# A gated linear attention and two MLPs on one core: halves of 64 tokens, another order of the first transfers, measured durations in the planner

## The chip, the core and the metric

The kernel runs on one core of a Trainium2 chip. The metric is device time in microseconds (us) from one launch. TensorE (PE) multiplies; VectorE (DVE) and ScalarE (ACT) do the elementwise work; SyncE (SP) issues every transfer, in program order. Each engine executes its own instructions in the order in which they were written down for it, and waits on semaphores for the others.

## What is computed

```python
def _attn_ref(q, k, v, f_logit) -> np.ndarray:
    B, H, S, D = q.shape
    f = 1.0 / (1.0 + np.exp(-f_logit))
    state = np.zeros((B, H, D, D), dtype=np.float32)
    y = np.zeros_like(q)
    for t in range(S):
        state = f[:, :, t, :, None] * state + np.einsum('bhd,bhe->bhde', k[:, :, t], v[:, :, t])
        y[:, :, t] = np.einsum('bhd,bhde->bhe', q[:, :, t], state)
    return y.astype(np.float32)
...
def _moe_ref(x, w_in, w_out) -> np.ndarray:
    h = x @ w_in
    relu6 = np.clip(h + 3.0, 0.0, 6.0)
    g = h * relu6 / 6.0
    return (g @ w_out).astype(np.float32)
...
    attn_out = _attn_ref(**attn_kwargs)
    B, H, S, D = attn_out.shape
    x = np.ascontiguousarray(attn_out.transpose(0, 2, 1, 3)).reshape(B * S, H * D)
    x = _moe_ref(x=x, **moe_kwargs)
    return _moe2_ref(x=x, **moe2_kwargs)
```

B, H, S, D are 4, 8, 768, 48. The second MLP has `h * tanh(softplus(h))` between its two products. Both have 3072 tokens, 384 features and 2048 hidden units. The data are float32; the weights arrive as float64.

## The kernel before

The attention runs in 24 units `u` of 128 tokens of one batch (six units to a batch, so units 0, 6, 12 and 18 start with an empty state and units 5, 11, 17 and 23 have no successor). The eight heads stand in four pairs `p`, one head of a pair in partitions 0 to 47 and the other in 64 to 111. `attention` (L232) makes of a unit: decay logs (`exp`, `ln` on ACT, L249, L251), their running sums (for units 0 to 7 by matmuls with the triangle `tri`, `sum_up`, L258; for the others by a scan on DVE, L266), the scaled `k` and `q` (L269, L271), `scores` (L277: 8 matmuls of 128 columns, 48 rows deep), the masked scores `A` (L286), the transposed `k` (`turn`, L296, copied to `kn`), `outer` (L303: 16 matmuls of 48 columns, the product of k and v that goes into the state), and `values` (L320): 12 matmuls of 128 columns that multiply `q` with the old state `sd`, and 16 that multiply the masked scores with `v`, on top of them in the same PSUM bank. In units from 4 on, `outer` stands inside `values`. `carry` (L338) brings the state `st` to the unit's end, two ACT copies (L348) put it into `sd`. The unit's output is split into a high and a low part, `xh` and `xl` (L352, L353).

The MLPs run on six blocks of 512 tokens (four units), first MLP over all blocks, then the second. For each of 16 hidden slices `f`, `hidden` (L363) does 9 large matmuls of 128x128 by 512 columns into `h` (three products of high and low parts for each of three feature tiles), an activation `g` split into `gh` and `gl`, and 9 more large matmuls into the three `o` banks. Each weight slice of the first MLP comes as 768 KB of float64 (`raw`), is turned into float32 by two ACT and two DVE operations (`stream`, L205) through a single buffer `we` (`WE = 1`), and split by ACT into `wh` and by DVE into `wl` (`weight`). This happens in the first block; the weights stay in memory. The second MLP's weights are converted later and written to DRAM.

The order of the work on every engine is made by a planner (`Plan.emit`, L111) when the program is built: it plays the operations through with an assumed cost for each and, on an engine that comes free, takes of the operations that are ready at that moment the one with the lowest rank. The costs are the numbers in `act`, `dve`, `dma` and `pe` (L181 to L192). Whatever it finds ready in an idle moment is written into the engine's order at that place, and has to be executed there. Where it sees PE idle before the first hidden slice, it puts in dummy matmuls on `cap` (`warm`).

## Time and profile before

| | us |
|---|---|
| median of 3 runs | 913.21 (912.27 to 915.97) |
| the profiled execution | 913.63 |
| its span, first to last instruction | 911.8 |
| PE busy | 894.3 |
| DVE busy | 645.2 |
| ACT busy | 554.7 |

The profiled execution is 1.8 us longer than its span. A busy PE is not PE at its peak: its rows overlap, so the text counts from the start of one matmul to the start of the next. The granted TensorE clock is 0.999 of full speed (2.4 GHz) over the span. The stages: up to 36.7 us the first four units of attention without any hidden slice (the head), up to about 123 us the first block with the stream of weights, up to about 460 us the other blocks of the first MLP with units 8 to 23 between them, and from there the second MLP.

### The profile page before, as it was taken

Reading aid. Unit: us, or ns where it says so; the run is one execution under the profiler, and the core shown is the slowest. Engines: PE = TensorE matmul, PEld = TensorE weight load, DVE = VectorE, ACT = ScalarE, POOL = GpSimd, SP = SyncE. Lnnn points to the kernel's source line nnn. Section 1 sums busy time; section 2 is a strip of 40 time slices with the busy share of each in tenths; the row PEclk is TensorE's granted clock in tenths of the full one; section 3 lists DMA queues with packets and bytes.
Section 4 is the critical chain, followed back from the end, with each engine's and each line's share of the span. In section 5 each row is a group of like instructions: output and inputs, shape, how many; then the busy total and the mean of one; then the engine's idle time right before and its main releaser. Section 6 shows DMA issues by size and latency. Waiting matters only on the chain.

```text
span 911.8 us, 14717 instructions
## 1 busy us (share of the span) xinstructions
PE 894.3 (98%) x5945; PEld 732.8 (80%) x5945; DVE 645.2 (71%) x979; ACT 554.7 (61%) x943; POOL 0.2 (0%) x4
## 2 busy tenths in 40 slices
PE   9899899999999999999999999999999999999997
PEld 8777678888888878888888888888888888888785
DVE  3889977766655445543465878888888888876894
ACT  5888876757545444433454665766666666654673
POOL 0000000000000000000000000000000000000000
PEclk9999999999999999999999999999999999999999
DMA  9756656656412111200233300200100100000001
GB/s 267 221 183 207 199 176 230 202 194 230 135 55 77 52 44 42 79 13 1 72 103 93 116 1 1 70 1 6 65 1 12 58 1 13 35 1 0 36 1 38
DMA packets 30155, 75.86 MB, mean 83 GB/s; under 512 B 3456, under 2 KB 4736, under 8 KB 30080
## 3 DMA queue, kind: packets, MB, share of 16 engines
q1 hardware_dynamic: 30080, 74.86, 25.7%
q8 instruction: 48, 0.79, 0.4%
q14 instruction: 27, 0.22, 0.1%
HBM read 59.11 MB, written 15.73 MB: 82 GB/s over the span
## 4 chain that ended last, share of the span: by engine, by line
PE 89%; DVE 4%; ACT 3%; DMA 3%; issue 1%; SPq 0%; ACTq 0%
PE o L196 42%; PE h L196 28%; PE a L196 14%; PE m L196 5%; DMA raw<-w 1%; DMA f<-fn 1%; DVE we L216 1%; DMA o<-fn 1%; PE m L298 1%; DVE we L218 1%; ACT f L183 1%; ACT we L183 1%; DVE wl L199 1%; DVE gl L199 0%; ACT raw L183 0%
## 5 line engine op out<-in xcount | busy, mean ns | idle before, releaser
L196 PE MATMUL o<-gl,wh 128*128 128x512 f32 x570 | 223.0, 391 | 5.1 <-DVE gl L199 5.1
L196 PE MATMUL o<-gh,wh 128*128 128x512 f32 x570 | 226.3, 397 | 0.1
L196 PE MATMUL o<-gh,wl 128*128 128x512 f32 x570 | 222.3, 390 | 0.0
L196 PE MATMUL h<-xh,wh 128*128 128x512 f32 x402 | 158.3, 394 | 0.0
L196 PE MATMUL h<-xh,wl 128*128 128x512 f32 x402 | 156.7, 390 | 0.0
L196 PE MATMUL h<-xl,wh 128*128 128x512 f32 x402 | 156.5, 389 | 0.0
L391 DVE SCALAR_TENSOR_TENSOR g<-g,h 128x512 f32<-128x512 f32 x96 | 65.9, 686 | 117.6 <-ACT g L183 117.5
L196 PEld LDWEIGHTS o<-gl,wh 128*128 128x128 f32 x570 | 107.0, 188 | 28.8 <-DVE gl L199 7.8
L196 PEld LDWEIGHTS o<-gh,wh 128*128 128x128 f32 x570 | 107.0, 188 | 27.0 <-issue 3.0
L196 PEld LDWEIGHTS o<-gh,wl 128*128 128x128 f32 x570 | 107.0, 188 | 22.4
L183 ACT ACTIVATE g<-h,small 128x512 f32<-128x512 f32 x96 | 65.8, 686 | 96.8 <-PE h L196 91.9
L183 ACT ACTIVATE gh<-q 128x512 fp32r<-128x512 f32 x94 | 59.3, 631 | 75.1 <-DVE q L202 71.2
L183 ACT ACTIVATE gh<-g 128x512 fp32r<-128x512 f32 x96 | 60.5, 630 | 50.8 <-DVE g L391 50.8
L196 PEld LDWEIGHTS h<-xh,wl 128*128 128x128 f32 x402 | 75.5, 188 | 16.2 <-DVE wl L199 0.2
L196 PEld LDWEIGHTS h<-xh,wh 128*128 128x128 f32 x402 | 75.5, 188 | 15.9 <-issue 0.6
L199 DVE TENSOR_TENSOR gl<-g,gh 128x512 fp32r<-128x512 f32 x96 | 66.1, 689 | 30.6 <-ACT gh L183 30.1
L196 PEld LDWEIGHTS h<-xl,wh 128*128 128x128 f32 x402 | 75.5, 188 | 15.2
L183 ACT ACTIVATE q<-k,small 128x512 f32<-128x512 f32 x96 | 69.4, 723 | 19.5 <-DVE k L399 16.4
L183 ACT ACTIVATE k<-k 128x512 f32<-128x512 f32 x96 | 59.5, 625 | 32.4 <-DVE k L396 32.4
L202 DVE TENSOR_TENSOR q<-q,k 128x512 f32<-128x512 f32 x96 | 66.0, 688 | 15.3 <-ACT q L183 13.7
L199 DVE TENSOR_TENSOR gl<-q,gh 128x512 fp32r<-128x512 f32 x94 | 64.6, 688 | 7.7 <-ACT gh L183 6.8
L399 DVE SCALAR_TENSOR_TENSOR k<-k 128x512 f32<-128x512 f32 x96 | 65.3, 685 | 0.8 <-ACT k L183 0.7
(130 smaller groups left out, 1154.9 us busy)
## 6 DMA issues: line engine op xcount, KB each, us to landing
raw<-w SPq DMA_DIRECT2D x32, 768.0 KB, 4.6
v<-vn SPq DMA_DIRECT2D x24, 256.0 KB, 3.0
w<-we SPq DMA_DIRECT2D x16, 384.0 KB, 2.6
raw<-w SPq DMA_DIRECT2D x16, 384.0 KB, 3.0
k<-kt SPq DMA_DIRECT2D x23, 224.0 KB, 3.0
q<-qt SPq DMA_DIRECT2D x23, 224.0 KB, 3.6
x<-o SPq DMA_DIRECT2D x18, 256.0 KB, 2.3
f<-x SPq DMA_DIRECT2D x18, 256.0 KB, 2.7
```

The source lines that it names most:

```text
L183: lambda: nc.scalar.activation(out=out(), in_=in_(), func=func, **k), r, w)
L196: nc.tensor.matmul(**k)
L199: dve(n, rank, lambda: nc.vector.tensor_tensor(out=out(), in0=a(), in1=b().bitcast(F32), op=ALU.subtract), r, w)
L202: dve(n, rank, lambda: nc.vector.tensor_tensor(out=out(), in0=a(), in1=b(), op=ALU.mult), r, w)
L216: dve(768, rank, lambda: stt(out=eu(), in0=eu(), scalar=3, in1=v(0), op0=ALU.logical_shift_left, op1=ALU.bitwise_or), (e, raw, (raw, 0)), ...
L218: dve(768, rank, lambda: stt(out=eu(), in0=v(1), scalar=0x80000000, in1=eu(), op0=ALU.bitwise_and, op1=ALU.bitwise_or), (e, raw), (e,))
L298: nc.tensor.transpose(ztv()[:, p, :], k3()[:, p, :], ident[0:R, 0:R])
L391: dve(n, rank, lambda: nc.vector.scalar_tensor_tensor(out=gg(), in0=gg(), scalar=6.0, in1=zn(), op0=ALU.min, op1=ALU.mult), (g, z), (g,))
L399: dve(n, rank, lambda: nc.vector.scalar_tensor_tensor(out=ee(), in0=ee(), scalar=2.0, in1=ee(), op0=ALU.add, op1=ALU.mult), (e,), (e,))
```

## The change

Units from 8 on (`SPLIT`) are worked in two halves of 64 tokens. The scores are formed within each half only: 16 matmuls of 64 columns. The scaled `q` of one head and the masked scores of the same head stand above each other in the partitions of one tile `T` (`A`), and the state and `v` above each other in `v`, so that one matmul over up to 128 partitions gives both terms: `values` is 32 matmuls of 64 columns and the 12 of the state are gone. The second half needs the state in the middle of the unit: `outer` runs twice (32 matmuls; once in a last unit, which had none), with a copy of `v` whose second half is zero, and `middle` (two DVE operations) adds it to the state. The outer products now stand behind the scores in the same PE operation. The mask becomes four DVE operations of 64x256 in place of two of 128x512, the scaled `q` two in place of one. A last unit now also has a `turn`. New inputs are `vs` (512 KB a unit in place of 256 KB) and `vk` (384 KB a unit).

The first 21 transfers have an order written out by hand (`FIRST`). The planner's costs are other numbers. Some tiles share memory in another way (`kh`, `kl` are gone; two `A` are one).

```diff
+SPLIT = 8
+CC = C // 2
...
-CST_RANK = -12
+FIRST = "f0 tri k0 q0 f1 f2 ident v0 k1 q1 f3 v1 w0 k2 q2 v2 k3 q3 w1 v3 w2".split()
...
-    sd = const.tile([R, NP, PD], F32, name="sd")
...
+    sd = new("vk", [128, 2 * NP * PD], 2)
+    sdv = lambda: sd()[0:R, 0:NP * PD].rearrange("p (a b) -> p a b", a=NP)
...
-        P.op("act", 0.065 + n / 1200 + (0.09 if "accum_out" in k or "bias" in k and k["bias"] != 1.0 else 0), rank,
+        P.op("act", max(0.36, 0.03 + n / 1000) + (0.22 if "accum_out" in k else 0.04 if k.get("bias", 1.0) != 1.0 else 0), rank,
...
-        P.op("dve", 0.065 + n / (1920 if fast else 960), rank, fn, r, w)
+        P.op("dve", max(0.38 if n > 128 else 0.1, 0.065 + n / 960), rank, fn, r, w)
...
-        P.op("sp", max(0.65, size / 360e3), rank, lambda: nc.sync.dma_start(out=out(), in_=in_()), r, w,
+        P.op("sp", max(0.45, size / 280e3), FIRST.index(name) - 99 if name in FIRST else rank, lambda: nc.sync.dma_start(out=out(), in_=in_()), r, w,
...
+        if split:
+            w = new("vk", [128, 2 * NP * PD], 2)
+            wv = lambda i: w().rearrange("p (i a d) -> p i a d", i=2, a=2 * NP)[:, i]
+            dma(rk(1), w, lambda: vk[u - SPLIT], (), (w,), 128 * 3072)
+            dma(rk(3), v, lambda: vs[u - SPLIT], (), (v,), 128 * 4096)
+        else:
+            dma(rk(3), lambda: v()[:, 0:NP * 128], lambda: vn[u], (), (v,), 128 * 2048, f"v{u}")
...
-            dve(512, rk(1), lambda: nc.vector.tensor_tensor_scan(out=bf(), data0=cap, data1=fl(f)(), initial=0.0,
+            dve(1024, rk(1), lambda: nc.vector.tensor_tensor_scan(out=bf(), data0=cap, data1=fl(f)(), initial=0.0,
...
+        if split:
+            T = new("A", [128, 2 * 2 * NP * CC], 2)
+            Tv = lambda: T().rearrange("p (i c a t) -> p i c a t", i=2, c=2, a=NP)
+            chunks = lambda z, r0, r1: z()[r0:r1].rearrange("p (a c t) -> p c a t", a=NP, c=2)
+            own, other = ((0, HB), (HB, R)), ((HB, 128), (0, HB))
+            cols = ((0, D), (CC - D, CC))
+            for i, (r0, r1) in enumerate(own):
+                dve(512, rk(2), lambda i=i, r0=r0, r1=r1: nc.vector.tensor_tensor(
+                    out=Tv()[r0:r1, i], in0=chunks(q, r0, r1), in1=chunks(lambda: bf(), r0, r1), op=ALU.mult),
+                    (q, b), ((T, "q", i),))
...
+            pe(0.4, rk(3), turn, (k, "ident"), (zt,))
+            act(448, rk(3.5), lambda: flat(kn()), lambda: flat(ztv()), AF.Copy, (zt,), (kn,))
+            zs = [bank("a", [128, 512], 2) for i in range(2)]
+
+            def scores():
                 for p in range(NP):
+                    for c in range(2):
+                        t = slice(c * CC, c * CC + CC)
+                        for i, (r0, r1) in enumerate(SPANS):
+                            mm(out=zs[i]()[t, p * CC:(p + 1) * CC], lhsT=k3()[r0:r1, p, t], rhs=Tv()[r0:r1, i, c, p],
+                               start=True, stop=True)
+                for p in range(NP):
+                    for m in range(1 if last else 2):
+                        for g in range(0, R, 32):
+                            to = slice(g, min(g + 32, R))
+                            mm(out=zuv(m)[to, p, :], lhsT=kn()[:, p, to], rhs=wv(1 - m)[:, 2 * p + (g >= HB)],
...
+            pe(1.1, rk(4), scores, (k, kn, w, (T, "q", 0), (T, "q", 1)), (*zs, zu))
             if not first:
+                for i, (r0, r1) in enumerate(own):
+                    act(192, rk(3), lambda i=i, r0=r0, r1=r1: vv()[r0:r1, i, 0, :, cols[i][0]:cols[i][1]],
+                        lambda r0=r0, r1=r1: st[r0:r1], AF.Copy, ("st", v), ((v, 0, i),))
+            for i, (r0, r1) in enumerate(own):
+                def middle(i=i, r0=r0, r1=r1):
+                    to = vv()[r0:r1, i, 1, :, cols[i][0]:cols[i][1]]
+                    if first:
+                        nc.vector.tensor_copy(out=to, in_=zuv(0)[r0:r1])
+                    else:
+                        nc.vector.tensor_tensor(out=to, in0=st[r0:r1], in1=zuv(0)[r0:r1], op=ALU.add)
+
+                dve(192, rk(5), middle, (zu, v, *(() if first else ("st",))), ((v, 1, i),))
+            for c in range(2):
+                for i in range(2):
+                    def mask(i=i, c=c):
+                        t = slice(c * CC, c * CC + CC)
+                        nc.vector.tensor_tensor(
+                            out=Tv()[other[i][0]:other[i][1], i, c],
+                            in0=zs[i]()[t, 0:NP * CC].rearrange("p (a t) -> p a t", a=NP),
+                            in1=tri[t, t].unsqueeze(1).to_broadcast([CC, NP, CC]), op=ALU.mult)
+
+                    dve(256, rk(5.5 + c), mask, (zs[i], "tri"), ((T, i, c),))
...
+            zx = bank("a", [128, 512], 2)
...
+            def values():
+                for w in range(2):
+                    for c in range(2):
+                        for n in range(w, 3 * NP, 1 + 2 * w):
+                            p, j = divmod(n, 3)
+                            i, at = ((0, 0), (0, 32), (1, 32))[j] if not w else (1, 0)
+                            mm(out=zxv()[n % 4 * 32:n % 4 * 32 + 32, n // 4, c * CC:(c + 1) * CC],
+                               lhsT=vv()[0:(128, R)[i], i, c, p, at:at + 32], rhs=Tv()[0:(128, R)[i], i, c, p],
+                               start=(not w and not c and n < 4), stop=(j != 1 or w == 1), skip_group_check=True)
+
+            pe(1.0, rk(7), values, (v, *(((v, 0, i) for i in range(2)) if not first else ()), (v, 1, 0), (v, 1, 1),
+                                    (T, "q", 0), (T, "q", 1), *((T, i, c) for i in range(2) for c in range(2))), (zx,))
...
+        else:
+            mul(512, rk(2), fl(q), fl(q), bf, (q, b), (q,))
...
-        pe(9 * (0.003 + n / 2400), i - TAIL_LEAD * tail, run, [("w", f, 0), ("w", f, 1), *x_keys(ph, j, 0), *x_keys(ph, j, 1)], (z,))
+        pe(9 * (0.0135 + n / 2400), i - TAIL_LEAD * tail, run, [("w", f, 0), ("w", f, 1), *x_keys(ph, j, 0), *x_keys(ph, j, 1)], (z,))
...
-            gs = [new(f"k{p}", [128, 512], 1, F32R) if tail and f == NF - 2 else new(f"g{p}", [128, 512], 3, F32R)
+            gs = [new("f", [128, 512], 2, F32R) if tail and f == NF - 2 else new(f"g{p}", [128, 512], 3, F32R)
...
-            pe(3 * (0.003 + n / 2400), i + 1.5 + m * 0.01, run, (("w", f, 0), ("w", f, 1), *gs, *((zo,) if f else ())),
+            pe(3 * (0.0135 + n / 2400), i + 1.5 + m * 0.01, run, (("w", f, 0), ("w", f, 1), *gs, *((zo,) if f else ())),
...
+    vk = np.zeros((NU - SPLIT, C, 2, NP, 2, D), v.dtype)
+    vk[:, :, 0, :, 0] = vn[SPLIT:, ..., 0:D]
+    vk[:, :, 0, :, 1] = vn[SPLIT:, ..., 128 - D:128]
+    vk[:, :CC, 1] = vk[:, :CC, 0]
+    vs = np.zeros((NU - SPLIT, 128, 2, 2, NP, HB), v.dtype)
+    for c in range(2):
+        t = slice(c * CC, c * CC + CC)
+        vs[:, CC:, 0, c] = vn[SPLIT:, t, :, 0:HB]
+        vs[:, :CC, 1, c] = vn[SPLIT:, t, :, HB:128]
...
```

SP, the first transfers of the program (`f`, `k`, `q`, `v` of units 0 to 3; the first two `o` are the `f` of units 2 and 3). Before:

```order
L189 DMA f<-fn 128x448
L189 DMA k<-kt 112x512
L189 DMA f<-fn 128x448
L189 DMA q<-qt 112x512
L189 DMA k<-kt 112x512
L189 DMA o<-fn 128x448
L189 DMA tri<-cst 128x128
L189 DMA q<-qt 112x512
L189 DMA ident<-cst 128x128
L189 DMA k<-kt 112x512
L189 DMA o<-fn 128x448
```

And in the changed program:

```order
L192 DMA f<-fn 128x448
L192 DMA tri<-cst 128x128
L192 DMA k<-kt 112x512
L192 DMA q<-qt 112x512
L192 DMA f<-fn 128x448
L192 DMA o<-fn 128x448
L192 DMA ident<-cst 128x128
L192 DMA v<-vn 128x512
L192 DMA k<-kt 112x512
L192 DMA q<-qt 112x512
L192 DMA o<-fn 128x448
```

`tri` went from seventh to second, `k` and `q` of unit 0 stand before the `f` of unit 1, and the `k` of unit 2 has left this piece.

DVE, one turn of the weight loop late in the first block, from one `g` to the next (`we` and `wl` are the weight's, `b` is the scan). Before:

```order
L391 SCALAR_TENSOR_TENSOR g<-g,h 128x512
L202 TENSOR_TENSOR q<-q,b 112x512
L266 SCALAR_TENSOR_TENSOR b<-cap,f 112x512
L216 SCALAR_TENSOR_TENSOR we<-we,raw 128x768
L218 SCALAR_TENSOR_TENSOR we<-raw,we 128x768
L199 TENSOR_TENSOR gl<-g,gh 128x512
L286 TENSOR_TENSOR A<-a,tri 128x512 x2
L199 TENSOR_TENSOR wl_120<-we,wh_119 128x768
L391 SCALAR_TENSOR_TENSOR g<-g,h 128x512
```

And in the changed program:

```order
L494 SCALAR_TENSOR_TENSOR g<-g,h 128x512
L289 TENSOR_TENSOR A<-q,b 48x512
L277 SCALAR_TENSOR_TENSOR b<-cap,f 112x512
L219 SCALAR_TENSOR_TENSOR we<-we,raw 128x768
L221 SCALAR_TENSOR_TENSOR we<-raw,we 128x768
L202 TENSOR_TENSOR gl<-g,gh 128x512
L330 TENSOR_TENSOR v<-st,m 64x4x48
L330 TENSOR_TENSOR v<-st,m 48x4x48
L337 TENSOR_TENSOR A<-a,tri 64x256
L202 TENSOR_TENSOR wl_119<-we,wh_118 128x768
L494 SCALAR_TENSOR_TENSOR g<-g,h 128x512
```

The turn still holds attention operations ahead of `wl`; they are now those of unit 8, `middle` and the small masks.

PE, a `values` between a hidden slice and output matmuls (`q,sd` is the state's part, `A,v` the scores'). Before:

```order
L196 MATMUL h<-xh,wh_121 128x512
L196 MATMUL h<-xl,wh_121 128x512
L196 MATMUL h<-xh,wl_122 128x512
L196 MATMUL a<-q,sd 32x128 x12
L196 MATMUL a<-A,v 32x128 x16
L196 MATMUL o_1651<-gh,wh_119 128x512
```

And in the changed program:

```order
L199 MATMUL h<-xh,wh_120 128x512
L199 MATMUL h<-xl,wh_120 128x512
L199 MATMUL h<-xh,wl_121 128x512
L199 MATMUL a<-A,v 32x64 x32
L299 MATMUL m<-ident,k 128x112 x4
L199 MATMUL o_710<-gh,wh_118 128x512
```

The 28 matmuls of 128 columns became 32 of 64, and the next unit's `turn` stands right behind them.

## Rows read from the trace of the kernel before

**Rows 1.** The page, busy time by engine: us (share) xinstructions.

```profile
PE 894.3 (98%) x5945; PEld 732.8 (80%) x5945; DVE 645.2 (71%) x979; ACT 554.7 (61%) x943; POOL 0.2 (0%) x4
```

**Rows 2.** Busy time by window: start:end length, then each engine's us, clock, DMA.

```profile
100.00:122.00 22.00, 18.37 (x131) 13.71 (x119) 19.12 (x27) 18.26 (x32) 0.00 (x0) 1.00 0.52 169
...
300.00:460.00 160.00, 160.00 (x1253) 129.94 (x1253) 73.91 (x117) 66.37 (x118) 0.00 (x0) 1.00 0.14 43
```

**Rows 3.** Waits of PE, 37 to 126 us: us in total, times, longest.

```profile
PE o L196 <- DVE gl L199: 5.1, 6, 1.6
```

**Rows 4.** Timeline of PE, attention pieces: start, us, what, xrecords (two a matmul).

```profile
38.97 0.54 PE L196 MATMUL m<-v,kn 128*32 128x48 f32 x32
39.33 0.83 PE L196 MATMUL a<-q,sd 112*32 112x128 f32 x24
39.99 1.05 PE L196 MATMUL a<-A,v 128*32 128x128 f32 x32
40.97 0.50 PE L196 MATMUL h<-xh,wh 128*128 128x512 f32 x1
...
47.77 1.03 PE L196 MATMUL m<-tri,f 128*112 128x128 f32 x8
48.56 0.47 PE L196 MATMUL o<-gh,wh 128*128 128x512 f32 x1
...
53.38 1.16 PE L196 MATMUL a<-q,k 48*128 48x128 f32 x16
54.47 1.13 PE L196 MATMUL m<-tri,f 128*112 128x128 f32 x8
55.35 0.47 PE L196 MATMUL o<-gh,wh 128*128 128x512 f32 x1
...
302.32 0.39 PE L196 MATMUL o<-gh,wl 128*128 128x512 f32 x1
302.64 1.16 PE L196 MATMUL a<-q,k 48*128 48x128 f32 x16
303.74 0.50 PE L196 MATMUL o<-gh,wh 128*128 128x512 f32 x1
...
325.45 0.55 PE L298 MATMUL m<-ident,k 112*128 112x112 f32 x4
325.77 0.47 PE L196 MATMUL h<-xh,wh 128*128 128x512 f32 x1
```

**Rows 5.** Timeline of PE in the head.

```profile
1.59 8.16 PE L196 MATMUL o<-cap 112*112 112x128 f32 x52 [1.59 <-DVE small L447]
9.84 1.10 PE L196 MATMUL o<-tri,f 128*112 128x128 f32 x8
...
15.32 1.13 PE L196 MATMUL o<-tri,o 128*112 128x128 f32 x8 [0.50 <-ACT b L183]
...
36.68 0.50 PE L196 MATMUL h<-xh,wh 128*128 128x512 f32 x1
```

**Rows 6.** The chain that ended last, first 60 us: start, us, what.

```profile
26.59 1.63 issue
...
57.68 2.04 PE h L196 x9
```

**Rows 7.** Timeline of DVE, the low part of a weight slice in the first block.

```profile
37.99 0.95 DVE L199 TENSOR_TENSOR wl<-we,wh 128x768 fp32r<-128x768 f32 x1
...
116.99 0.96 DVE L199 TENSOR_TENSOR wl<-we,wh 128x768 fp32r<-128x768 f32 x1 [0.31 <-ACT wh L183]
...
121.87 0.96 DVE L199 TENSOR_TENSOR wl<-we,wh 128x768 fp32r<-128x768 f32 x1 [0.40 <-ACT wh L183]
```

**Rows 8.** Groups of DVE instructions: xcount, busy us, mean ns, idle before.

```profile
L286 DVE TENSOR_TENSOR A<-a,tri 128x512 f32<-128x512 f32 x44 | 28.7, 684 | 5.3 <-PE a L196 5.3
...
L343 DVE TENSOR_TENSOR st<-st,m 112x192 f32<-112x192 f32 x13 | 4.5, 349 | 0.0
```

**Rows 9.** Timeline of PE in the last block of the second MLP.

```profile
854.29 0.50 PE L196 MATMUL m<-xh,wh 128*128 128x512 f32 x1 [1.34 <-DVE q L202]
```

More of the change, by code (lines that the diff above doesn't have):

```diff
@@ L156, in emit, with fast_path @@
                 o.fn()
-def fast_path(ctx, tc, qt, kt, ft, fn, vn, w1, w2, cst, ident, flag, w2_d, out):
+def fast_path(ctx, tc, qt, kt, ft, fn, vn, vs, vk, w1, w2, cst, ident, flag, w2_d, out):
     nc = tc.nc
@@ L236, in attention @@
         third = early and u == 3
+        split = u >= SPLIT
         f, k, q = (new(nm, [128, 512], bufs) for nm, bufs in (
-            ("o", 3) if early and u > 1 else ("f", 2), ("kh", 1) if third else ("k", 3), ("kl", 1) if third else ("q", 3)))
-        v = new("v", [128, NP * 128], 3)
+            ("o", 3) if early and u > 1 else ("f", 2), ("k", 3), ("q", 3)))
+        v = new("v", [128, 2 * NP * 128], 3)
+        vv = lambda: v().rearrange("p (i c a d) -> p i c a d", i=2, c=2, a=NP)
         view = lambda z: lambda: z()[0:R].rearrange("p (a b) -> p a b", a=NP)
@@ L270, in attention @@
         act(512, rk(1), bf, logs, AF.Exp, (zk,), (b,), scale=-1.0)
-        mul(512, rk(2), fl(q), fl(q), bf, (q, b), (q,))
-        A = [new(nm, [128, 4, C], bufs) for nm, bufs in (
-            (("gl", 3), ("gl", 3)) if early and u == 1 else (("gl", 3), ("g", 1)) if third else (("A", 2), ("A", 2)))]
-        head = lambda p, i: A[i]()[:, p]
-        zs = [bank("a", [128, 512], 2) for i in range(2)]
-        def scores():
-            for p in range(NP):
-                for i, (r0, r1) in enumerate(SPANS):
-                    mm(out=zs[i]()[:, p * C:(p + 1) * C], lhsT=k3()[r0:r1, p, :], rhs=q3()[r0:r1, p, :], start=True,
-                       stop=True)
-        pe(1.1, rk(4), scores, (k, q), zs)
-        for i in range(2):
-            def mask(i=i):
-                nc.vector.tensor_tensor(out=A[i](), in0=zs[i]().rearrange("p (a c) -> p a c", a=4),
-                                        in1=tri.unsqueeze(1).to_broadcast([128, 4, C]), op=ALU.mult)
-            dve(512, rk(5 + i), mask, (zs[i], "tri"), (A[i],))
-        if not last:
-            zt, zu = bank("m", [128, 512], 1), bank("o0" if early else "m", [128, 512], 1)
+        if split:
[8 more added lines that the diff above has]
+                    (q, b), ((T, "q", i),))
+            zt, zu = bank("m", [128, 512], 1), bank("m", [128, 512], 1)
             kn = new("kn", [128, NP, R], 1)
             ztv = lambda: zt()[:, 0:NP * R].rearrange("p (a b) -> p a b", a=NP)
-            zuv = lambda: zu()[:, 0:NP * D].rearrange("p (a b) -> p a b", a=NP)
+            zuv = lambda i: zu()[:, i * NP * D:(i + 1) * NP * D].rearrange("p (a b) -> p a b", a=NP)
             def turn():
@@ L304, in outer @@
                 for p in range(NP):
-                    for g in range(0, R, 32):
-                        at = p * 128 + (0 if g < HB else 128 - D)
-                        mm(out=zuv()[g:min(g + 32, R), p, :], lhsT=kn()[:, p, g:min(g + 32, R)],
-                           rhs=v()[:, at:at + D], start=True, stop=True)
-            if early:
-                pe(0.6, rk(7), outer, (kn, v), (zu,))
-        zx = bank("h" if early else "a", [128, 512], 2)
-        zxv = lambda: zx()[:, 0:KC * C].rearrange("p (a b) -> p a b", a=KC)
@@ L315, in strip @@
-        def strip(n):
-            return zxv()[n % 4 * 32:n % 4 * 32 + 32, n // 4, :]
-        joint = not (early or last)
-        def values():
-            if joint:
-                outer()
-            if not first:
-                for n in range(3 * NP):
-                    p, j = divmod(n, 3)
-                    mm(out=strip(n), lhsT=sd[:, p, j * 32:j * 32 + 32], rhs=q3()[:, p, :], start=(n < 4), stop=False,
-                       skip_group_check=True)
-            for w in range(2):
-                for n in range(w, 3 * NP, 1 + 2 * w):
-                    p, j = divmod(n, 3)
-                    at, i = ((0, 0), (32, 0), (96, 1))[j] if not w else (64, 1)
-                    mm(out=strip(n), lhsT=v()[:, p * 128 + at:p * 128 + at + 32], rhs=head(p, i),
-                       start=(first and not w and n < 4), stop=(j != 1 or w == 1), skip_group_check=True)
@@ new lines, in attention, with carry @@
+            if not last:
+                def carry():
+                    fv = b()[:, :, C - 1:C].to_broadcast([R, NP, D])
+                    if first:
+                        nc.vector.tensor_tensor(out=st, in0=zuv(1)[0:R], in1=fv, op=ALU.mult)
+                    else:
+                        nc.vector.tensor_tensor(out=st, in0=st, in1=zuv(1)[0:R], op=ALU.add)
+                        nc.vector.tensor_tensor(out=st, in0=st, in1=fv, op=ALU.mult)
+                P.op("dve", 0.38 if first else 0.77, rk(6.7), carry, (zu, b, "st"), ("st",))
```

122 lines of the change are left out of this document (90 added, 32 removed).

## The prediction

> **What bounds the kernel now.** I read the busy times first: PE is busy 98% of the span, DVE 71%, ACT 61% [rows 1]. So an edit is worth the PE time that it removes, or a wait of PE that it ends. I then went through the starts of PE's large matmuls. Nine of them in a row take 2.04 us, 0.227 each [rows 6], and there are 3,456 of them, 783 us that the change leaves alone. The rest of the 911.8 us is in four places.
>
> The head: the first large matmul starts at 36.68 us [rows 5]. The attention pieces between the hidden slices, which I price by the distance between the large matmuls before and after them. The waits of PE: 5.1 us in six pieces between 37 and 126 us, all for `gl` of DVE [rows 3], where DVE is busy 19.1 of 22 us [rows 2]; the reader is to see that in this stretch alone another engine than PE sets the pace. And one wait of 1.34 us in the last block [rows 9]. From 300 to 460 us PE has no gap and DVE 74 of 160 us of work [rows 2]. The profiled execution took 913.63 us, its span plus 1.8; it lies 0.4 above the median of 913.21, and I make the sum against 913.63.
>
> **The pieces on PE, before.** All from [rows 4]. `scores`: from 302.32 to 303.74 is 1.42, less 0.23 for the large matmul itself, 1.19 us; of that 0.09 is on entering (0.32 to its start instead of 0.23), and 1.10 are 16 records and the way out. They run as 8 pairs (two heads, two halves of the array's rows), about 0.112 a pair of 128 columns, so the way out is about 0.2. `turn`: 0.32. `outer` with `values`: `outer` 0.36, state 0.66, masked scores 0.98 to the next large matmul, and 0.10 for entering, 2.10 us. A unit thus costs 1.19 + 0.32 + 2.10 = 3.61 us, a first one (no state) 2.95, a last one (no `turn`, no `outer`) 2.93.
>
> **The pieces on PE, after.** The rows come in sets of four, one for each strip of 32 columns. The state's 24 records are six sets in 0.66, so 0.110 a set of 128 columns; `outer`'s 32 are eight sets in 0.36, 0.045 a set of 48. On the line between the two a set of 64 columns takes 0.058. `values` is then 64 records, 16 sets, 0.93, and with 0.10 in and 0.11 out 1.14 us in place of 1.74. `outer` twice is 0.72 (0.36 in a last unit). No row shows the new scores, 64x64 tiles. If four of them run side by side, as the strips do, 32 records are eight sets, 0.46; if only the two row halves do, as now, 16 sets, 0.93. I take 0.46, because it is the full array that is in use either way, and keep 0.93 for the range. Scores and `outer` now stand in one piece. Does that save an entry? The row where sums follow scores says no: from 53.38 to 55.35 is 1.97, while scores alone are 1.10 and sums alone (47.77 to 48.56) 0.79, so changing from one shape to the next costs both ways plus 0.08. The piece is then scores 0.09 + 0.46 + 0.20, `outer` 0.10 + 0.72 + 0.11, and 0.08, together 1.76; 1.5 if the change of shape came free.
>
> A unit is 1.76 + 0.32 + 1.14 = 3.22, 0.39 less than before; a first one 3.22 against 2.95, 0.27 more; a last one 2.86 against 2.93, 0.07 less. There are eleven, two and three of them from unit 8 on: -4.3 + 0.5 - 0.2 = **-4.0 us** (between -8.2 with free changes of shape and +3.5 with scores in pairs).
>
> **The head.** The first sums start at 9.84, right behind 52 records of dummy matmuls from 1.59 on [rows 5], which is where `tri`, seventh in the queue, had landed. After the change 15 dummies stand there, 30 records; at the mean pace of the 52 they end at 6.3, and to be on the safe side I take 6.9 for the start of the sums, 2.9 earlier. But the sums of unit 2 came at 15.32 [rows 5] and are now behind unit 0's `outer` and `values`; I walk there by the prices above: sums at 6.9, 2.3 for two exponentials, 0.6 for the product, scores at 10.5, unit 1's sums, `outer` of unit 0 and, after the two masks, `values`, so 14.4. From there to the first hidden slice the order holds on PE three sums (0.95 each), three `turn`s (0.48), three scores (1.1), three `outer` (0.37), three `values` with state (1.65) and twelve dummies (0.21), 16.2 us, so 30.6; DVE, which waits for `k` and `q` of unit 3 (they now stand behind a weight slice and two `v` in the queue), adds 0.8 by my estimate. PE also stood 1.63 us in the middle of an `outer` with no releaser [rows 6]; I count 1.1 for such stalls. First large matmul at 32.5, **-4.2 us** (0 if the later `k` and `q` hold everything up, -5.3 without stalls). `turn` and scores of unit 4 stood ahead of it and now stand behind it: **+1.5**.
>
> **The weight loop of the first block.** Buffer `we` is single, so ACT's copy of slice f+1 waits for DVE's `wl` of slice f, and the four steps go round in a ring. Undisturbed a turn takes 4.88 us (116.99 to 121.87), but from slice 1 (37.99) to slice 15 (121.87) the 14 turns take 83.9, or 5.99 each [rows 7]: attention operations that the planner put into the ring, because it took DVE for idle, hold it up, and PE ends up waiting. The new order still puts attention in there. Counted over the same 14 turns, DVE has for units 8 to 10 six scaled `q` halves (0.6 each, 3.6) in place of three wholes (1.8), four small masks and two `middle`. For the small masks the nearest rows are 0.68 for 512 columns and 0.35 for 192 [rows 8], between them 0.36 net of overlap; the sum is +1.8 + 1.4 + 0.7 = 3.9 us. About 1 us of DVE work in each of a turn's two gaps is free, since ACT is at work then; of the 3.9 I count 1.2. With slice 1 ready at 34.4, some 2 us after the first large matmul as before, slice 15 is ready at 34.4 + 85.1 = 119.5 in place of 122.8. PE's own work up to there was 122.8 + 0.9 - 36.7 = 87.0, less its waits: 5.1 and, since the row of the matmul ahead (0.39) runs 0.16 past the next one's due start and the pace needs one more matmul to come back, some 0.26 for each of the six, 6.7. To these 80.3 come `turn` and scores of unit 4 (1.5) and all of unit 8 (3.2), so PE alone would be there at 32.5 + 85.0 = 117.5. About 2 us of waits are left: **-4.7** (0 to -6.7).
>
> **What goes along.** DVE has per unit 1.5 us more (halved `q` +0.6, masks +0.24, `middle` +0.66), 24 us in all; ACT the same, and a `kn` copy in each last unit. It lies beside PE from 123 us on, in the idle half of DVE [rows 2]; its price without that cover is a rival below. The transfers grow by 640 KB a unit, 10 MB over a stretch in which the DMA engines are 14% busy from 300 us on [rows 2]; they sit on SP behind weight transfers that wait for DVE, and a late `v` now also stops ACT's copy of the state and every `g` behind it. I see them three units ahead (three buffers of `v`, two of `vk`) and count nothing. The wait in the last block [rows 9] comes from an order planned with matmuls at 0.216 in place of 0.227; half of it, **-0.8** (0 to -1.5).
>
> **Sum:** 913.6 - 4.2 + 1.5 - 4.7 - 4.0 - 0.8 = 901.4, and as a median 0.4 less: **901 us**.
>
> **Rivals.** (A) The ring keeps its waits: all 3.9 us of added DVE work lands in it, slice 15 is ready at 122.2, and 2.7 come back, 903.7; for it, the order still shows attention inside the turns; against it, the planner's costs are now close to the rows. (B) The head gains little, since unit 3's `k` and `q` come later and the first large matmul is at 36: +3.5, 904.5. (C) Scores in pairs: +7.5, 908.5, on the edge of no measurable change. (D) Slower by records: a narrow matmul's record costs what a wide one's does. Then scores are 32 records of 0.068, 2.18, `values` 64 of 0.029, 1.86; a unit is 3.48 + 0.32 + 2.07 = 5.87, 2.26 more than before, 38 us over the 16 units instead of the gain of 4, 943. It decides where the pieces of a unit cost over 4.1 us, because 8.2 us of other gains over 16 units are 0.51 each. Against it, `outer`'s records follow each other in 0.36/32 = 11 ns where the 128-column ones take 28 [rows 4]. The Trainium skill ("TensorE: Matmul & The Clock Gate", section "Wait — 56ns, not 53.3ns?") says that starts of matmuls never come closer than about 25 ns, however few the columns; by that a unit would be about 5.1 us and the kernel, as an estimate, some 930. By that rule the 11 ns could not be, and the trace decides against it for strips of 32 columns. (E) Slower by DVE: between scores and `values` one hidden slice and one output slice stand, 4.08 us, and DVE has to do `middle` and four masks (2.1), `g` and `gl` (1.2), and where a weight conversion falls in (1.9) that is 5.2; 1.1 a unit over 16 units is +18, 919. It decides from 0.8 us a unit. Against it, only half of the units have a conversion there, and DVE is half idle.
>
> **How the numbers follow.** Chances: forecast 0.54, A 0.16, B 0.10, C 0.10, D 0.04, E 0.06. A measurement of this kernel tells a change from none at about 0.5%, 4.6 us, so faster means under 908.6: forecast, A and B, 0.80; within 0.5%: C, 0.10; slower, D and E, 0.10. The range goes down to 893 (changes of shape free, -4.2; no waits left in the first block, -2; no stalls in the head, -1.1, and a little) and up to 910 (C, with part of A).
>
> **What would show it.** First large matmul at 32 to 34 us; slice 15's `wl` near 119; a piece of scores and `outer` 1.7 to 1.8 between its neighbours, `values` 1.1; PE's waits for `gl` at about 2 us; no waits of PE between 130 and 460. The prediction is wrong if score records come in pairs 0.058 apart, if `values` waits for a mask in unit after unit, or if the head still ends at 36.

## The result, and the profile after

The changed kernel takes 906.01 us (median of 4 runs, 905.27 to 907.7) and the kernel before 913.65 in the runs beside it: a ratio of 0.9913 (95% interval 0.9892 to 0.9933), 0.9% faster. The forecast was 901, its range 893 to 910. The profiled execution took 907.7, its span 905.9, so 5.9 us less than the span before; the forecast's sum for it was 901.4.

The busy times, against [rows 1]: PE lost 7.3 us, DVE gained 31.4. The two windows of [rows 2] follow; columns as there.

```profile
PE 887.0 (98%) x6905; PEld 726.0 (80%) x6905; DVE 676.6 (75%) x1059; ACT 551.6 (61%) x946; POOL 0.2 (0%) x4
```

```profile
100.00:122.00 22.00, 16.82 (x130) 12.20 (x130) 20.78 (x29) 17.68 (x31) 0.00 (x0) 1.00 0.60 199
300.00:460.00 160.00, 160.00 (x1661) 130.06 (x1659) 89.14 (x153) 66.80 (x119) 0.00 (x0) 1.00 0.21 64
```

Behind the first block nothing waits: PE has no gap in 160 us, although DVE has 15 us more to do there. At the end of the first block DVE is busy 20.78 of 22 us (19.12 before), and PE only 16.82 (18.37 before). The waits of PE there, against [rows 3]:

```profile
PE o L199 <- DVE gl L202: 6.4, 7, 1.6
PE h L199 <- DVE wl L202: 0.3, 1, 0.3
```

5.1 us became 6.7. The attention pieces on PE behind unit 8, against [rows 4] (timeline of PE: start, us, what, records):

```profile
316.11 0.55 PE L299 MATMUL m<-ident,k 112*128 112x112 f32 x4
316.43 0.48 PE L199 MATMUL h<-xh,wh 128*128 128x512 f32 x1
...
318.36 0.39 PE L199 MATMUL h<-xh,wl 128*128 128x512 f32 x1
318.68 0.69 PE L199 MATMUL a<-A,k 48*64 48x64 f32 x32
319.30 0.88 PE L199 MATMUL m<-vk,kn 128*32 128x48 f32 x64
320.11 0.50 PE L199 MATMUL o<-gh,wh 128*128 128x512 f32 x1
...
324.11 0.39 PE L199 MATMUL h<-xh,wl 128*128 128x512 f32 x1
324.43 1.11 PE L199 MATMUL a<-A,v 128*32 128x64 f32 x64
325.46 0.50 PE L199 MATMUL o<-gh,wh 128*128 128x512 f32 x1
```

From one neighbour to the other, less 0.23 for the large matmul itself: scores with `outer` 1.75 - 0.23 = 1.52, `turn` 0.32 (from its start to the next large matmul), `values` 1.35 - 0.23 = 1.12. A unit costs 1.52 + 0.32 + 1.12 = 2.96 us, where it cost 3.61. The head, against [rows 5]:

```profile
1.59 5.14 PE L199 MATMUL o<-cap 112*112 112x128 f32 x30 [1.59 <-DVE small L550]
6.57 1.04 PE L199 MATMUL o<-tri,f 128*112 128x128 f32 x8
...
25.47 0.29 PE L199 MATMUL o<-v,kn 128*32 128x48 f32 x8 [1.23 <-issue]
...
31.39 0.30 PE L199 MATMUL h<-gl,v 128*32 128x128 f32 x2 [1.59 <-issue]
...
34.37 0.48 PE L199 MATMUL h<-xh,wh 128*128 128x512 f32 x1
```

The first sums are 3.3 us earlier, the first large matmul 2.3; PE stands 2.8 us in two places with nothing that it waits for. The low part of weight slices 1 and 15 on DVE, against [rows 7]:

```profile
35.75 0.96 DVE L202 TENSOR_TENSOR wl<-we,wh 128x768 fp32r<-128x768 f32 x1
...
122.04 0.96 DVE L202 TENSOR_TENSOR wl<-we,wh 128x768 fp32r<-128x768 f32 x1 [0.53 <-ACT wh L186]
```

Slice 1 is 2.2 us earlier and slice 15 0.2 later: the 14 turns take 86.3 us (6.16 each) where they took 83.9 (5.99). So the weight loop gave back all that the head had gained.

**Where the 5.9 us of the span come from**, by the distances between PE's large matmuls: the head -2.3; all attention pieces behind it -6.3 (-7.8 by the smaller pieces of units 8 to 23, +1.5 because `turn` and scores of unit 4 came behind the first large matmul); pauses between large matmuls that follow each other (what their starts are apart beyond 0.227 us) +2.4, of which 1.5 in the first block; the end of the program +0.3.

### The profile page after: what moved, and what is told of

It reads as the page before. It is cut to its first block, busy times and chain, and to the rows that moved or that the text cites. A ratio compares the mean times of both kernels' runs of the same rounds, so it can differ in the third digit from the quotient of the medians.

```text
span 905.9 us, 16770 instructions
## 1 busy us (share of the span) xinstructions
PE 887.0 (98%) x6905; PEld 726.0 (80%) x6905; DVE 676.6 (75%) x1059; ACT 551.6 (61%) x946; POOL 0.2 (0%) x4
## 4 chain that ended last, share of the span: by engine, by line
PE 93%; DVE 4%; issue 1%; ACT 1%; DVEq 0%
PE o L199 44%; PE h L199 29%; PE a L199 13%; PE m L199 6%; DVE we L219 1%; PE m L299 1%; DVE we L221 1%; DVE gl L202 0%; DVE wl L202 0%; DVE A L289 0%; DVE g L494 0%; PE m L401 0%; DVE b L277 0%; DVE q L205 0%; DVE k L205 0%
```

## The experiments

All kernels here are the changed one with an edit (`again` has none), and compute everything. The kernel before, run beside them, had medians between 912.8 and 913.3. The table counts DVE's work in the 14 turns of the weight loop from its order and the durations of the rows; "turns" is the time from slice 1's low part to slice 15's; "first" is PE's first large matmul; the ratio is to the kernel before. The intervals are some 2 us wide to either side, so rows that lie closer than that are told apart by their traces and not by the medians. "First" holds pauses of PE for which the profile shows no cause: 2.6 us in the kernel before, 2.8 in the changed one's first profile, 2.3 in `both5`, 2.0 in `ramp`, 1.9 in `oldcost`, none in the others.

| | median us | ratio (95%) | first | DVE work | turns |
|---|---|---|---|---|---|
| before | 913.65 | 1 | 36.7 | 74.6 | 83.9 |
| the change | 906.01 | 0.9913 (0.9892 to 0.9933) | 34.4 | 78.5 | 86.3 |
| again | 905.32 | 0.9919 (0.9901 to 0.9937) | 31.5 | 78.5 | 87.0 |
| gate | 902.35 | 0.9895 (0.9875 to 0.9915) | 31.2 | 69.3 | 79.1 |
| we2 | 901.08 | 0.9868 (0.9846 to 0.9890) | 32.1 | 70.8 | 78.0 |
| both5 | 899.52 | 0.9853 (0.9831 to 0.9874) | 34.5 | 67.2 | 74.1 |
| ramp | 897.14 | 0.9825 (0.9806 to 0.9845) | 35.1 | 67.2 | 74.6 |
| nosplit | 909.82 | 0.9975 (0.9965 to 0.9985) | 31.8 | 75.8 | 83.1 |
| nosplit_both | 905.92 | 0.9919 (0.9900 to 0.9937) | 32.9 | 67.2 | 72.8 |
| oldboth | 908.91 | 0.9960 (0.9947 to 0.9974) | 35.3 | 77.9 | 86.5 |
| oldfirst | 909.34 | 0.9958 (0.9942 to 0.9975) | 33.9 | 77.3 | 86.1 |
| oldcost | 907.80 | 0.9942 (0.9922 to 0.9962) | 35.9 | 77.3 | 87.0 |
| sep | 904.78 | 0.9910 (0.9890 to 0.9931) | 31.4 | 81.9 | 88.0 |

### The weight loop: gate and we2

My theory after the result was that the loop had absorbed the head's gain and part of the pieces'; the rival, that its time is tied to something else. `gate` keeps attention of units from 8 on out of the loop, by a dependency that only the planner sees:

```diff
-                                                                 op0=ALU.min, op1=ALU.add), (f, "cap"), (b,))
+                                                                 op0=ALU.min, op1=ALU.add), (f, "cap", ("w", NF - 2, 1)), (b,))
```

> The whole of the changed kernel; only the planner is told that the scan of units from 8 on may not begin before DVE's low part of weight slice 14, so that no attention of these units is written into the weight ring of the first block. DVE's work in the 14 turns from slice 1 to slice 15 falls from 78.5 to about 69.3 us. Theory (the ring gave back what the head and the pieces gained): a turn falls from 6.16 to about 5.5 us, slice 15's low part starts near 113 instead of 122.0, PE's waits for gl fall from 6.4 to under 2 us; PE then starts the second block without unit 8's pieces (3 us, which come later), and the kernel takes about 901.5 (6.4 us of waits and some 2 us of slow starts behind them, less 4 that a ring near PE's own pace leaves). Rival (the ring is tied to PE and not to DVE, or what is taken out of it makes PE wait behind it): slice 15 moves, but waits of the same size show up elsewhere, 905 to 908.

It took 902.35. Waits of PE from 31 to 126 us, and on DVE the turn from the low part of slice 12 to that of slice 13:

```profile
PE o L199 <- DVE gl L202: 3.7, 6, 1.1
```

```profile
96.21 0.96 DVE L202 TENSOR_TENSOR wl<-we,wh 128x768 fp32r<-128x768 f32 x1 [0.36 <-ACT wh L186]
97.08 0.68 DVE L494 SCALAR_TENSOR_TENSOR g<-g,h 128x512 f32<-128x512 f32 x1
98.13 0.96 DVE L219 SCALAR_TENSOR_TENSOR we<-we,raw 128x768 uint32<-128x768 uint32 x1 [0.36 <-ACT we L186]
99.12 0.96 DVE L221 SCALAR_TENSOR_TENSOR we<-raw,we 128x768 uint32<-128x768 uint32 x1
100.00 0.68 DVE L202 TENSOR_TENSOR gl<-g,gh 128x512 fp32r<-128x512 f32 x1
101.17 0.96 DVE L202 TENSOR_TENSOR wl<-we,wh 128x768 fp32r<-128x768 f32 x1 [0.49 <-ACT wh L186]
```

That turn takes 4.96 us. In the changed kernel the same turn, with `k`, both halves of `q` and the scan in it, takes 7.10:

```profile
104.00 0.95 DVE L202 TENSOR_TENSOR wl<-we,wh 128x768 fp32r<-128x768 f32 x1
104.87 0.68 DVE L205 TENSOR_TENSOR k<-k,f 112x512 f32<-112x512 f32 x1
105.47 0.68 DVE L494 SCALAR_TENSOR_TENSOR g<-g,h 128x512 f32<-128x512 f32 x1
106.07 0.68 DVE L289 TENSOR_TENSOR A<-q,b 64x512 f32<-64x512 f32 x1
106.67 0.94 DVE L219 SCALAR_TENSOR_TENSOR we<-we,raw 128x768 uint32<-128x768 uint32 x1
107.65 0.96 DVE L221 SCALAR_TENSOR_TENSOR we<-raw,we 128x768 uint32<-128x768 uint32 x1
108.52 0.69 DVE L202 TENSOR_TENSOR gl<-g,gh 128x512 fp32r<-128x512 f32 x1
109.24 0.69 DVE L289 TENSOR_TENSOR A<-q,b 48x512 f32<-48x512 f32 x1
109.96 1.23 DVE L277 TENSOR_TENSOR_SCAN b<-cap,f 112x512 f32<-112x512 f32 x1
111.10 0.93 DVE L202 TENSOR_TENSOR wl<-we,wh 128x768 fp32r<-128x768 f32 x1
```

In that piece DVE never waits. The four attention operations take 3.1 us from start to start, and the turn is 2.1 longer: what is free is what DVE waits in the turn without them, 0.36 + 0.49 = 0.85 us, and the rest counts. Over the whole loop, 9.2 us of work less in the loop made the 14 turns 7.2 shorter. By the medians the kernel is 3 to 4 us faster; by the ratios it is 1.6 to 2.2, inside the intervals, and from the first large matmul to the last its profile is 3.4 to 4.5 us shorter than the changed kernel's two. 3.7 us of waits stay. Three of the six, 0.4 to 0.6 us each, stand between 95 and 106 us, where the loop is empty of attention: its own turn of 4.8 to 5.0 us is longer than the 4.08 in which PE does a slice. The longest, 1.1 us at 111, is in the last turn, in which three operations of unit 8 stand behind the low part of slice 14. The theory held; its figure for the waits (under 2) did not.

`we2` gives the float32 weight a second buffer:

```diff
-WE = 1
+WE = 2
...
-        v = new("v", [128, 2 * NP * 128], 3)
+        v = new("v", [128, 2 * NP * 128], 2)
```

> The whole of the changed kernel, with two buffers of the float32 weight instead of one (and two of v instead of three, to make room). ACT's copy of the next slice then no longer waits for DVE's low part of the last one. Theory (it is the single buffer that ties ACT and DVE into a ring): PE's waits for gl in the first block fall from 6.4 to under 2 us and the kernel takes about 901 to 902. Rival (it is DVE's load alone, 94% busy at the end of the block): DVE has the same work per slice, the waits keep 5 us or more, 905 to 907; the two buffers of v would show as PE waits for v behind 126 us.

It took 901.08, and no `gl` is waited for any more; the largest wait from 32 to 126 us is of another kind (two of 0.6 us are left out):

```profile
PE h L199 <- ACT wh L186: 2.6, 1, 2.6
```

So the waits were the loop's. By itself it does not tell the second buffer from a lighter loop, since the planner also wrote 7.7 us less work into it. `both5` below, which has both edits, does: there the turns without attention take 4.3 to 4.4 us (89.34 to 93.76, 99.65 to 103.97) where those of `gate` take 4.8 to 5.0, and no `gl` is waited for.

### The halves alone, and without them: oldboth, nosplit, nosplit_both

`oldboth` keeps the halves and takes the order of the first transfers and the costs from before (the minus lines of the diff in `act`, `dve`, `dma` and `pe`), with

```diff
-FIRST = "f0 tri k0 q0 f1 f2 ident v0 k1 q1 f3 v1 w0 k2 q2 v2 k3 q3 w1 v3 w2".split()
+FIRST = []
+CST_RANK = -12
```

In turn, `nosplit` keeps order and costs and works all units in one piece:

```diff
-SPLIT = 8
+SPLIT = NU
```

> The halves alone: the order of the first transfers and the costs of the planner are those of before. If the halves earn their 7.7 us whatever stands around them: 913.4 - 7.7 plus up to 2 us of more waits in the weight ring (DVE has 77.9 us of work there against 74.6 before), 905.5 to 908; the first large matmul is back near 36.7. That would mean that the new order and costs add nothing to the end time. If the gain of 2.3 us in the head counts in full, 908 to 910.

> The changed kernel without halves: all 24 units in one piece of 128 tokens as before; the new order of the first transfers and the new costs of the planner stay. If the pieces on PE are worth the 7.7 us that the two traces give (3.61 against 2.98 us a unit), it takes 906 + 7.7 less up to 2 us, because DVE has 2.7 us less to do in the weight ring: 911.5 to 914. If they are worth the 4.0 of the prediction: 908 to 910.

908.91 and 909.82. `oldboth` lies where the head was to count in full, though its first large matmul came at 35.3 and not near 36.7. `nosplit` missed its 911.5 to 914 and lies where the pieces were to be worth 4.0. By the end time the halves are worth 3.8 to 4.5 us (909.82 against 906.01 and 905.32; 5 to 6 by the ratios), and alone they bring 0.4%. Yet in `nosplit` the attention pieces between large matmuls sum to 70.4 us, 8.1 more than in the changed kernel's first profile. The rest is found in the loop, which holds 2.7 us less of DVE's work without unit 8's halves; the waits of `nosplit` from 31 to 126 us:

```profile
PE o L199 <- DVE gl L202: 3.6, 5, 1.3
```

3.6 where the changed kernel has 6.4 and 5.5 (second profile); pauses between adjacent large matmuls are 14.6 us in all, against 19.1 and 19.6. The halves save about 8 us of PE and hand some half of it back as pauses. `nosplit_both` asks for the same with the loop out of the way (both edits above, no halves), beside `both5` below, which has the halves and another lead in the last block; the wait there is the same in both, 1.35 and 1.33 us:

> All 24 units in one piece as before (no halves), with the two changes to the weight ring: no attention of units from 8 on in it, and two buffers of the float32 weight. Beside the same ring with halves (899.5) it shows what the halves are worth at the end when the ring does not stand in between. If the 7.7 us that the pieces save on PE then count in full: 907.2. If something else holds the end, as with the old ring (909.8 against 905.7, 4.1 us): 903.5.

905.92 against 899.52: 6.4 us, and 6.6 between the first and the last large matmul of the two profiles, where the pieces differ by 7.1. With the loop freed most of it counts, nearer to the 907.2 than to the 903.5 of the expectation.

### The first transfers and the costs: oldfirst, oldcost

`oldfirst` takes only the order of the transfers from before (the diff of `oldboth` above, `CST_RANK` included), `oldcost` only the costs, as here and with the multipliers of 0.003 in `hidden` and the output slices:

```diff
-        P.op("dve", max(0.38 if n > 128 else 0.1, 0.065 + n / 960), rank, fn, r, w)
+        P.op("dve", 0.065 + n / 960, rank, fn, r, w)
```

> The changed kernel, with the transfers in the order of before (the triangle seventh); halves and new costs stay. First sums back to about 9.3, first large matmul without stalls at 34 (31.5 with the new order). If the weight ring sets the end of the first block (DVE 77.3 us of work in it), only part of the 2.5 us is seen in the time: 906 to 907.5. If the head counts in full: 908.5.

909.34, above both expectations: with the new costs the order of the transfers is worth 3.3 to 4 us, more than the 2.4 of the head. Its first sums and its waits (33 to 130 us):

```profile
10.62 1.04 PE L200 MATMUL o<-tri,f 128*112 128x128 f32 x8
```

```profile
PE o L200 <- DVE gl L203: 9.7, 9, 1.9
```

With the old order the low part of weight slice 1 starts at 38.5 instead of 33.1 (second profile), so the loop also starts late and PE waits 9.7 us for it. So with the new costs the new order moves not only the head but the start of the loop that bounds the first block. It is not the old order alone that does this: `oldboth` has it too, with the old costs, and there slice 1 starts at 34.9, no `gl` is waited for (the largest waits are 2.8 us for `wl` and 1.3 for `wh`), and the time is about the same, 908.91.

> The changed kernel, with the planner's costs of before; halves and the new order of transfers stay. If the new costs serve the end time, by fewer waits in the first block (DVE has 77.3 us of work in the ring here, 78.5 with the new costs), it is slower than 906, by 1 to 3 us. If they don't, since they leave more attention in the ring than the old ones: 904.5 to 906.

907.80, about 2 us slower than with the new costs, as expected, with 7.3 us of waits for `gl`. The two edits do not add up: the new order is worth 1.1 us with the old costs (908.91 to 907.80) and 3.3 to 4 with the new ones; the new costs are worth about 2 with the new order and nothing with the old one. Only the 3.3 to 4 stand clear of the medians' noise. In `oldcost`'s profile a stall of 1.9 us in the head is followed by a granted clock of 0.63 between 34 and 40 us, where TensorE stood at its lower level of 1.2 GHz for most of the time (columns as in [rows 2]):

```profile
34.00:40.00 6.00, 6.00 (x71) 4.82 (x71) 3.08 (x5) 3.19 (x7) 0.00 (x0) 0.63 0.64 217
```

So part of that one execution's time is not the order's; how much of the 2 us of the medians is, stays open.

### The same kernel once more: again

> The changed kernel itself, profiled a second time on the chip of the other runs. Theory (PE's two stalls without a releaser in the head, 2.8 us, are chance of an execution): they are gone or stand elsewhere, the first large matmul starts between 31.5 and 34.4, and the ring takes up the difference: slice 15's low part stays near 122 less what slice 1 comes earlier, and the time stays within 1 us of 906. Rival (they belong to the code): the same 1.2 and 1.6 us behind the same matmuls, first large matmul at 34.4.

905.32. The first large matmul in this second profile:

```profile
31.51 0.48 PE L199 MATMUL h<-xh,wh 128*128 128x512 f32 x1
```

and slice 15's low part:

```profile
120.05 0.96 DVE L202 TENSOR_TENSOR wl<-we,wh 128x768 fp32r<-128x768 f32 x1 [0.31 <-ACT wh L186]
```

No stall, and the head ends 2.9 us earlier; slice 15 is 2.0 earlier, the span 2.0 shorter. The stalls belong to an execution and not to the code. The second profile may be of another chip, but `both5`, on the chip of the second profile, has such stalls (0.7 and 1.6 us, ending at 25.37 and 31.67).

### Scores and outer apart: sep

`outer` becomes a PE operation of its own with a rank behind the scores:

```diff
-            pe(1.1, rk(4), scores, (k, kn, w, (T, "q", 0), (T, "q", 1)), (*zs, zu))
+            pe(0.6, rk(4), scores, (k, (T, "q", 0), (T, "q", 1)), zs)
+            pe(0.8, rk(4) + 0.01, outer, (kn, w), (zu,))
```

> The changed kernel, with the outer products as a PE operation of their own that comes after the scores, where the planner finds room. By the prediction's prices scores alone are 0.75 us between their neighbours and outer alone 0.93 (0.57 in a last unit), 1.68 together and less than the 1.76 that it gave them in one piece. If its way out was counted twice for the scores, these alone are 0.64. Joined the trace has 1.53. The time says little, since the order on DVE changes too: 904 to 908.

904.78, no different from the changed kernel. The planner put other work between the two only in two units. Scores alone in the one, `outer` alone in the other:

```profile
137.00 0.39 PE L199 MATMUL o<-gh,wl 128*128 128x512 f32 x1
137.31 0.69 PE L199 MATMUL a<-A,k 48*64 48x64 f32 x32
137.94 0.50 PE L199 MATMUL h<-xh,wh 128*128 128x512 f32 x1
```

```profile
108.93 0.39 PE L199 MATMUL o<-gh,wl 128*128 128x512 f32 x1
109.25 0.88 PE L199 MATMUL m<-vk,kn 128*32 128x48 f32 x64
110.06 0.50 PE L199 MATMUL h<-xh,wh 128*128 128x512 f32 x1
```

0.94 - 0.23 = 0.71 and 1.13 - 0.23 = 0.90, near the 0.75 and 0.93 of the prediction; the sum, 1.61, is 0.09 more than the joint piece. Joining saves 0.09, where the prediction added 0.08.

### A version that beats both: both5 and ramp

`both5` has the edits of `gate` and `we2`, and a lead of 5 in place of 6 for the last block's hidden slices (`HOLD, TAIL_LEAD = 14, 5`); `ramp` has both edits, the lead of 6, and lets it grow slowly:

```diff
-        pe(9 * (0.0135 + n / 2400), i - TAIL_LEAD * tail, run, [("w", f, 0), ("w", f, 1), *x_keys(ph, j, 0), *x_keys(ph, j, 1)], (z,))
+        pe(9 * (0.0135 + n / 2400), i - min(TAIL_LEAD, 0.5 * (f - NF + HOLD + 1)) * tail, run, [("w", f, 0), ("w", f, 1), *x_keys(ph, j, 0), *x_keys(ph, j, 1)], (z,))
```

> The changed kernel with both changes to the weight ring (no attention of units from 8 on in it, and two buffers of the float32 weight; DVE's work in the 14 turns is 67.2 us), and in the last block the hidden slices go 5 ahead of the output slices instead of 6. If the two changes remove the same waits, it is no faster than the second alone, 900 to 901; if each has waits of its own (3.7 and 3.8 us were left), 898 to 899.5. The last block: if its wait of 1.73 us comes from how far the hidden slices run ahead there, it changes by a us or more; if not, it stays 1.7.

> The changed kernel with both changes to the weight ring (as in the run before it, which took 899.5), the hidden slices of the last block again up to 6 ahead of the output slices, but the lead grows by half a slice with each slice instead of at once. Theory: the wait of 1.73 us for the m bank in the last block comes from hidden slices that follow each other faster than DVE and ACT take them out of their banks; it goes, and the kernel takes about 898. Rival: the wait has another place or comes later, 899.5.

`both5` took 899.52, and its waits for `gl` are gone. The last block's wait stayed (the expectations' 1.73 us is the distance from the start of the matmul ahead, 846.22 to 847.95). First the changed kernel (it answers to [rows 9]; in `both5` the same wait, 1.33 us, stands at 840.80), then `ramp` at the first use of the `m` bank in that stretch, without a wait:

```profile
847.95 0.50 PE L199 MATMUL m<-xh,wh 128*128 128x512 f32 x1 [1.34 <-DVE q L205]
```

```profile
843.52 0.39 PE L199 MATMUL m<-xh,wh 128*128 128x512 f32 x1
```

In `ramp` no matmul waits in the last block, and it takes 897.14, 1.75% less than the kernel before. Its 2.4 us against `both5` are more than the wait, and the intervals overlap; from the first large matmul to the last the two profiles differ by 0.7 us. So how much `ramp` is worth in time stays open; where the wait came from does not. It came from hidden slices one right after another, faster than DVE empties the bank; how far they lead in the end does not matter.

## Why the prediction was right, and where it was not

The sign and the range held, but in part by luck: against the sum's 901.4, the profiled execution came out 6.3 us later, and it would have been 10 without a term that missed the other way (the weight loop +7.1, the head +1.9, the last block +0.8, the end of the program +0.3; the pieces -3.8).

**The weight loop (-4.7; measured +2.4).** This is the term that failed, in two steps. The first is PE's own work, to which the prediction added `turn` and scores of unit 4 (1.5 us) and "all of unit 8 (3.2)". But unit 8 stood in the first block already. Its scores and the last part of its `values` before, and scores and `values` in the changed kernel:

```profile
94.85 1.16 PE L196 MATMUL a<-q,k 48*128 48x128 f32 x16
...
100.53 1.05 PE L196 MATMUL a<-A,v 128*32 128x128 f32 x32
```

```profile
94.41 0.69 PE L199 MATMUL a<-A,k 48*64 48x64 f32 x32
...
107.01 1.11 PE L199 MATMUL a<-A,v 128*32 128x64 f32 x64
```

Between the first large matmul and slice 15 all attention pieces together took 18.1 us before and 18.9 after, 0.8 more and not 4.7. With unit 8 counted once, PE's 117.5 becomes 32.5 + 80.3 + 1.5 - 0.4 = 113.9, and the loop at 119.5 leaves 5.6 us of waits in place of 2. The gain would have been about 1 us and not 4.7, by the prediction's own figures.

The second step is the loop itself, where rival A's mechanism is at work. The prediction counted 3.9 us of added work on DVE and let 1.2 of it through, because "about 1 us of DVE work in each of a turn's two gaps is free". The 14 turns grew by 2.4 us, and by 3.1 in the second profile; in `gate` they shrank by 7.2 for 9.2. The turn from `gate` shows both gaps together as 0.85 us, not 2; one attention operation of 0.6 us nearly fills them, and the further ones lengthen the turn. There is no fixed share, though: in `nosplit` 2.7 us less of work made the turns 3.2 shorter, and in `sep` 3.4 more made them only 1.7 longer. Counted as the prediction counts, at the end of its low part, slice 15 came at 123.0, where the forecast said 119.5 and rival A 122.2; 2.3 of the 3.5 us are the start of the loop (slice 1 at 36.7 and not 34.4, in the profile with the stalls), 1.2 the turns. In the second profile slice 1 came at 34.1 and slice 15 at 121.0.

Rival A still kept 2.0 of the 4.7 us; in fact the waits rose by 1.6, because PE reaches the block earlier with nearly the same work and has to wait for the same loop. Of the 2.4 us of pauses, 1.5 are in the first block (11.1 against 9.6); the rest lies behind it, 0.6 between 126 and 460 us and 0.2 in the last block, in no term of the prediction. The two experiments on the loop give back 3 to 5 us by the medians, and together about 6.

**The pieces on PE (-4.0; measured -7.8).** `turn` and `values` were right to 0.02 us, and scores come four at a time, as assumed: from 318.68 to the first `outer` at 319.30 are 0.62 us for 32 records of 64 columns, where pairs would need 0.93; in the trace the single records start in fours, 7 ns apart, one four every 58 ns. Rival C is out. The error is in the joint piece, 1.52 instead of 1.76. The 0.08 "for the change of shape" was read from a row in which sums follow scores, and there it was the entry of the sums; the price of `outer` held an entry already, so it was counted twice. And between these two shapes the change really saves 0.09 (`sep`). 0.24 over 16 units are the 3.8 us.

**The head (-4.2; measured -2.3).** Without stalls the walk gives 31.4, and the second profile shows 31.51. The stalls were the weak part: the walk counted 1.1, the first profile had 2.8 and the second none. The kernel before had 2.6 in its profile, so that like for like, both without stalls, the head is 36.7 - 2.6 = 34.1 against 31.5, -2.6 us. The prediction set 1.1 us of stalls against the 2.6 that were in its own reference. Rival B (first large matmul at 36) did not come about.

**Unit 4's turn and scores (+1.5)** were as said. **The last block (-0.8)** gave nothing: 1.34 us stand in both. The prediction's cause was the planner's price of a matmul, 0.216 in place of 0.227; with 0.227 the hidden slices followed each other as closely as before, and that was the cause (`ramp`).

**Rival D** (the price is by records) is refuted: `values` takes 1.03 us for 64 records, 16 ns each, where it asked for 1.86. The rule of the Trainium skill that the prediction named beside it ("TensorE: Matmul & The Clock Gate", section "Wait — 56ns, not 53.3ns?", no starts closer than about 25 ns) does not describe these records. Counted by the program's matmuls, two records each, `values` has 32 ns and would agree with it; the 16 matmuls of `outer` in 0.36 us [rows 4], 22 ns each, are under it either way. **Rival E** (DVE late between scores and `values`): no wait of PE between 130 and 460 us, and from 300 to 460 us DVE is busy 89 of 160.

## What to carry to other kernels

Where an engine's conversion loop sets the pace of a stage, price the operations written into it by the idle time that a turn has without them, whatever the engine's busy share over the program: 3.9 us of work on an engine that is 75% busy over the span made the loop 2.4 to 3.1 us longer, and the head's 2.3 us were gone when it ended. Before adding a unit's work to a stage, look whether it stands there already. And before adding up gains ahead of such a loop, ask when the loop itself starts and ends; what makes the other engine faster there turns into waiting. When a price is read from two operations in a row, mark which entry and exit each number holds, and count stalls on both sides of a comparison or on neither.

## What the runs showed of the hardware

PE stood still in the head in five of the thirteen profiles, 0.7 to 2.0 us at a time, at matmuls that waited for no engine and no transfer, and in the same program in one execution and not in another; in a sixth, `oldboth`, it did so for 1.7 us at 98 us. In the changed kernel the second stall ends at 31.39; shortly before, the DMA queue of instructions moved a packet, with the transfers' queue busy 96% (first profile, 28.5 to 30 us; share of 16 engines):

```profile
q1 hardware_dynamic: 274, 0.48, 96.3%
q8 instruction: 1, 0.02, 4.0%
```

That packet began at 29.1 us; in the second profile, which has no stall, the one that answers to it began at 25.2, with the transfers' queue at 27% (24 to 26 us). All eight stalls in the heads of the five profiles end 2.3 to 2.6 us after the start of such a packet; the one of `oldboth` at 98 us does not, the packet before it is 4.9 us away. That the instructions came late behind the transfers fits the eight, but this was only seen; no run varied it, so the cause stays open. It spreads the head of one kernel by up to 2.9 us, more than some of the terms of the sum.

A pause of PE can also cost more than its length. In four of the profiles the granted clock fell to 0.5 (1.2 GHz) inside the program, each time at a pause of 1.9 to 2.6 us: in `oldcost` at 31.7 us, in `ramp` at 26.0, in `we2` at 47.6, and in the second profile of the changed kernel at 101.3, where PE had just waited 1.85 us for `gl`. There the starts of the large matmuls from 101.67 to 104.65 are 0.43 us apart in place of 0.23, about 1.4 us in all. So its 19.6 us of pauses hold a piece that is the clock's, and the profiled executions of `we2` and `ramp` hold one too.
